# An attention-and-router kernel: overflow table built with the first constants, 16 buffers of row numbers, ranks after the state products, early row transposes in the last three rounds

## The chip, the cores and the metric

One Trainium2 chip, one of its cores. A core has a matrix engine (PE, its weight loads listed as PEld), a vector engine (DVE), a scalar engine (ACT), a general engine (POOL) and a sync engine (SP) that issues plain transfers; POOL issues the transfers that convert types or that go to rows named by an index. Each engine works off its own list of instructions in order. The metric is the device time of one execution in microseconds, lower is better; a change of 1% is about 2.7 us.

## The reference

Two stages. The first is linear attention with decay over 4 batches, 8 heads, 768 positions and 64 channels, worked in blocks of 64 positions:

```
intra = (qb @ kb^T * Dmask) @ vb
inter = (qb * lam_pow) @ kv_state
out[block] = intra + inter
kv_state = lam_block * kv_state + (kb * rev_pow)^T @ vb
```

Its output, transposed to 3072 tokens of 512 channels, is x of the second stage, a router with 8 experts:

```
logits = normalize(x) @ normalize(expert_emb).T / tau      # tau = 0.1
expert_idx = argmax(logits);  gate_w = softmax(logits)[expert_idx]
for e in range(8):                                         # w1[e]: 512x1024, w2[e]: 1024x512
    out[mask_e] = gate_w[mask_e] * (relu(x[mask_e] @ w1[e]) @ w2[e])
```

All inputs and the output are float32.

## The kernel before, in words

**Order.** The order of instructions on every engine is written out by hand (a manual schedule): the program text is walked once, and each engine gets its instructions in that order. Small steps of the router are hung into the attention rounds with `at(round, slot, step)`, and `run(i, slot)` puts them into the lists when round i comes to that slot. Semaphores are set by the framework where one engine needs another's result or buffer.

**Attention.** 24 rounds, i = 0 to 23, of 128 tokens each, six rounds to a batch. Round i transposes q and k for round i+2 (`pe_Tq`, `pe_Tk`), forms x against the embeddings for round i-1 (`pe_X`), forms the scores of round i+1 (`pe_ST`), and then fills the bank `o_ps` of round i: `pe_inter` (state times q, L354), `pe_kv` (the state's update, L380), `pe_O` (scores times v, L363). ACT copies the result to `xT` (`ev_O`), DVE updates the state, POOL scales k (`pool_ks`, L290). `o_ps` has one buffer, so the next round's `pe_inter` waits until every reader of the last `o_ps` is done.

**Router inside the rounds.** Tokens are ranked in eight groups, `[0..3] [4..7] [8..11] [12..15] [16,17] [18,19] [20,21] [22,23]`. For a group that ends at round n-1: one-hot choice `oh` on DVE in round n+1, then on PE the rank of each token within its expert (`pe_rank`: `ltri` and `ones` against `oh`, L469 to L474, into a free corner of `o_ps`), in round n+2 on DVE the row number (`rt_b`, L484 to L494), and then POOL scatters 128 rows at a time to a table in DRAM, `xs_dram` (`scatter`, L529). Once, after the first 16 tokens of rounds (`TA`), `pe_part` counts tokens per expert and `rt_part` (L504 to L508) turns the counts into a base for the later groups. `load_early` (round 20, on SP) then reads back the first 256 rows of the experts 0 to 2, after a small read `mark` that waits for the scatters of the first 16 rounds.

**Experts.** Rows come as three kinds: `a` (first 256 rows of the experts 0 to 2), `b` (their next 128), `f` (384 rows of the experts 3 to 7), and `q` (32 rows of each of four experts, in one block). For each piece PE transposes the rows (`xt_copy`, L598, copied to SBUF by ACT at L600; the last 32 columns by `add_q` on DVE, L735), then `pe_L1` (L753, relu by ACT at L755 and DVE at L757), then `pe_L2` (L787) whose result `put` scales on DVE into `y_sb` (L766). `put` first makes row numbers `xi` (`mask_rows`, L587, L589) and then POOL scatters `y_sb` to the output (L769). Order on PE: A0, A1, A2, B0, B1, B2, F3 to F7, with the `q` blocks between.

**Weights.** Each expert has four pieces of 512 KB in SBUF (float32 in DRAM, converted on the way), issued by POOL (`load_w`, L276), one list for all 32. Twelve are issued in the rounds, two more at the end of attention, and 18 between the output scatters, as the table `more` says. The first of these 18 stands behind `seen`, a copy on POOL that waits for rows of expert 3 (L779).

**Overflow.** `overs` (L807 to L818) makes from the counts a table of how many further tiles each expert needs; a branch at the very end reads it and does nothing here unless an expert has more than 416 rows. It starts with an `iota` on POOL, `pstart` (L807), which DVE reads at L813.

Of the kernel before, what the change touches and what calls it, by code (L numbers as in the profile page):

```python
# [11 lines left out]
FP32 = mybir.dt.float32  # L12
# [10 lines left out]
def kernel(  # L23
# [13 lines left out]
    P = 128  # L37
# [133 lines left out]
    lamb = const.tile([P, NC, HP], FP32, name="lamb")  # L171
    for c in range(NC):
        nc.vector.tensor_scalar(lamb[:, c, :], loglam_rows, float(c * 2 * P), None, op0=ALU.mult)
    lamq = const.tile([P, NC, 2, HP, P], FP32, name="lamq")

    def decays(c):
        for hp in range(HP):
# [49 lines left out]
    def last_constants():  # L227
        nc.gpsimd.memset(zrow, 0)
        nc.gpsimd.memset(zrow[:, :, DW : DW + 1], int(OOB_IDX))
        nc.gpsimd.tensor_copy(ident16, ident)  # L230
        nc.gpsimd.memset(ones16, 1.0)
        make_upper_triangular(nc, ltri, val=1.0, diag=False)
        nc.gpsimd.iota(rev, pattern=[[-1, E]], base=E, channel_multiplier=0,
                       allow_small_or_imprecise_dtypes=True)
        nc.gpsimd.iota(ebase[0], pattern=[[ROWS, E]], base=0, channel_multiplier=0,
                       allow_small_or_imprecise_dtypes=True)
        for t, n, base in ((row_a, 2, 0), (row_b, 1, CA), (row_f, GE, 0)):
            nc.gpsimd.iota(t, pattern=[[1, n]], base=base, channel_multiplier=n,
                           allow_small_or_imprecise_dtypes=True)
        for n in range(NQ):  # L240
            nc.gpsimd.iota(row_q[ds(CQ * n, CQ), :], pattern=[[0, 1]], base=GE * P,
                           channel_multiplier=1, allow_small_or_imprecise_dtypes=True)
        for n in range(4):
            nc.gpsimd.iota(tok_iota[ds(32 * n, 32), :], pattern=[[P, R]],
                           base=C * (n // 2) + n % 2, channel_multiplier=2)
        nc.gpsimd.memset(ohcum, 0.0)
        nc.gpsimd.memset(bump, 0.0)


    xps = ps2.tile([P, 2, 512], FP32, name="xps", tag="xps")  # L250
# [214 lines left out]
    def pe_rank(gi):  # L465
        nt = len(groups[gi])
        oh = rt[gi]["oh"]
        pc, pc3 = rank_of(gi)
        nc.tensor.matmul(pc, ltri, oh.rearrange("p k e -> p (k e)"), start=True, stop=False,  # L469
                         skip_group_check=True)  # L470
        nc.tensor.matmul(pc3, ones16, ohcum.unsqueeze(1).to_broadcast([P, nt, E]),
                         start=False, stop=(nt == 1), skip_group_check=True)
        for j in range(nt - 1):
            nc.tensor.matmul(pc3[:, j + 1 : nt, :], ones16,  # L474
                             oh[:, j : j + 1, :].to_broadcast([P, nt - 1 - j, E]),
                             start=False, stop=(j == nt - 2), skip_group_check=True)
# [16 lines left out]
        nc.vector.tensor_reduce(oc, d["oh"].rearrange("p k e -> p e k"), axis=AXL.X, op=ALU.add)  # L493
        nc.vector.tensor_tensor(ohcum, ohcum, oc, op=ALU.add)  # L494

    def pe_counts(dst):
        nc.tensor.matmul(dst, ones16, ohcum, start=True, stop=True, skip_group_check=True)

    def pe_part():
        pcs["a"] = bank["o"][:, 0, 2 * P + 64 : 2 * P + 64 + E]  # L500
        pe_counts(pcs["a"])

    def rt_part():
        nc.vector.tensor_copy(cnt_a, pcs["a"])  # L504
# [69 lines left out]
    def mask_rows(key):  # L574

        n = xe[key].shape[1]
        m = rsm.tile([P, GE], FP32, name="m", tag="m")[:, 0:n]
        kind, e = key
        if kind == "q":
            for r in range(NQ):  # L580
                nc.vector.tensor_scalar(m[ds(CQ * r, CQ)], row_q[ds(CQ * r, CQ), :],
                                        cnt[ds(CQ * r, CQ), NQ * e + r : NQ * e + r + 1], OOB_IDX,
                                        op0=ALU.is_ge, op1=ALU.mult)
        else:
            rows = {"a": row_a, "b": row_b, "f": row_f}[kind]
            c = cnt_a if kind == "a" else cnt
            nc.vector.tensor_scalar(m, rows, c[:, e : e + 1], OOB_IDX, op0=ALU.is_ge, op1=ALU.mult)  # L587
        xi[key] = rsm.tile([P, GE], I32, name="xi", tag="xi", bufs=4)
        nc.vector.tensor_tensor(xi[key][:, 0:n], xe[key][:, :, DW], m, op=ALU.max)  # L589

    def xt_copy(key, g0, g1, pst):
# [20 lines left out]
    for gi in range(GL):  # L612
# [3 lines left out]
        at(n + 1, "dve", rt_a2, gi)  # L616
        if groups[gi][0] == TA:
            at(n + 1, "pe", pe_part)
            at(n + 2, "dve", rt_part)
        at(n + 1, "pe", pe_rank, gi)  # L620
        if n + 2 < R:
            at(n + 2, "dve", rt_b, gi)
# [11 lines left out]
                at(min(n + 2 + late, R - 1), "pool", scatter, gi, j)  # L634
    at(0, "sp", fill)
    at(20, "sp", load_early)
    for i in (8, 10, 12, 14, 15, 16, 17, 20, 20, 21, 21, 22):
        at(i, "w", load_w, 1)

    def early_xT():  # L640
        xt_copy(("a", 0), 0, 2, ps.tile([P, DC * 2 * P], FP16, name="q_xtr", tag="q"))

    at(R - 2, "pe3", early_xT)

    act_q(0)
    pool_ks(0)
    for i in range(-2, R):
# [19 lines left out]
            ev_ST(i + 1)  # L667
        if i >= 0:
            new_o()
            run(i, "pe")  # L670
            pe_inter(i)
            pe_kv(i)
            pe_O(i)
            ev_O(i)
            state(i)
# [27 lines left out]
    mx = const.tile([P, 1], I32, name="mx")  # L703
    below = const.tile([P, E, R], FP32, name="below")
    ntile = const.tile([P, E], I32, name="ntile")
    pstart = const.tile([P, R], FP32, name="pstart")
    n_scat = [0]
    more = {1: 4, 2: 1, 3: 1, 4: 2, 5: 2, 6: 1, 7: 1, 8: 1, 9: 1, 11: 2, 12: 2}
    seen = const.tile([1, 1], I32, name="seen")
# [1 line left out]
    with (  # L711
        tc.tile_pool(name="wpool2", bufs=3) as wpool2,
        tc.tile_pool(name="moe_sb", bufs=2) as moe_sb,
        tc.tile_pool(name="moe_y", bufs=6) as moe_y,
        tc.tile_pool(name="ps_mx", bufs=1, space=bass.MemoryType.PSUM) as ps_mx,
        tc.tile_pool(name="ps_h", bufs=3, space=bass.MemoryType.PSUM) as ps_h,
        tc.tile_pool(name="ps_y", bufs=2, space=bass.MemoryType.PSUM) as ps_y,
# [42 lines left out]
        def put(y_ps, key, g):  # L760
# [15 lines left out]
            )  # L776

            if n_scat[0] == 1:
                nc.gpsimd.tensor_copy(seen, xe["f", NA][0:1, 0, DW : DW + 1])  # L779
            load_w(more.get(n_scat[0], 0))  # L780
            n_scat[0] += 1

# [21 lines left out]
            nc.vector.tensor_tensor(cnt, cp, bump, op=ALU.add)  # L804

        def overs():
            nc.gpsimd.iota(pstart, pattern=[[P, R]], base=0, channel_multiplier=0,  # L807
                           allow_small_or_imprecise_dtypes=True)
            nc.vector.tensor_scalar(last, cnt, -1.0, None, op0=ALU.add)
            nc.vector.tensor_scalar(over, cnt, float(-CE), 0.0, op0=ALU.add, op1=ALU.max)  # L810
            nc.vector.tensor_reduce(mx, over, axis=AXL.X, op=ALU.max)

            nc.vector.tensor_tensor(  # L813
                below, over.unsqueeze(2).to_broadcast([P, E, R]),
                pstart.unsqueeze(1).to_broadcast([P, E, R]), op=ALU.is_gt)
# [18 lines left out]
        rt_d(GL)  # L834
        for j in range(2):
            scatter(GL, j)
        for e in range(NA):
            load_b(e)
        load_xq(0)
        load_f(3)  # L840
        pe_xT(A[1], 0, 2)
        pe_L2(A[0], 0)
        counts()
        pe_L2(A[0], 1)
        pe_L1(A[1])
        pe_xT(A[2], 0, 2)
        pe_L2(A[1], 0)
        pe_L2(A[1], 1)
        pe_L1(A[2])
# [8 lines left out]
        for e in range(NA):  # L858
# [4 lines left out]
            else:  # L863
                pe_xT(F_[3], 0, 2)
            pe_L2(B_[e], 0)
        overs()
        pe_xT(F_[3], 2, 3)
        add_q(F_[3])
        for e in range(NA, E):
# [112 lines left out]
```

## Time and profile before

| what | value |
|---|---|
| time, median of 3 runs | 266.15 us (265.71 to 268.03) |
| profiled execution, own time | 263.92 us |
| its span | 262.0 us |
| PE busy | 221.4 us (84%) |
| DVE, ACT, POOL busy | 124.6, 127.6, 100.9 us |
| DMA | 49.76 MB, mean 190 GB/s |
| weight pieces | 32, 512 KB each in SBUF |

The profile shows one execution. Its own time is 1.92 us above its span, and 2.23 us under the median of the timed runs. A busy share is a mean over stages: attention runs to about 137 us, the experts from there to about 253 us, then the last output lands. In the rows below, an engine's idle time stands in brackets with the engine and the line that ended it.

### The profile page before, as it was taken

The numbers are of one execution on the slowest core, as the hardware profiler recorded it, in microseconds if no ns is written. First come the engines' busy times: TensorE is split into PE (matmuls) and PEld (weight loads), VectorE is DVE, ScalarE is ACT, GpSimd is POOL, SyncE is SP. The second block draws the span as 40 slices with busy tenths as digits, with TensorE's granted clock in tenths as the row PEclk, the third lists the DMA queues.
The fourth block names the chain that finished last, engine by engine and source line by source line (L and its number), as shares of the span: only waits on it lengthen the run. The fifth ranks groups of instructions, "written<-read, shape, count | busy, mean of one in ns | idle before, by whom it ended". The sixth has DMA issues, their size and how long they took to land.

```text
span 262.0 us, 7196 instructions
## 1 busy us (share of the span) xinstructions
PE 221.4 (84%) x2926; PEld 168.3 (64%) x2926; DVE 124.6 (48%) x413; ACT 127.6 (49%) x282; POOL 100.9 (39%) x143
## 2 busy tenths in 40 slices
PE   0799999997999997997889999970099999999960
PEld 0678897896888896886766776650045556565520
DVE  1274556657756667768744224531014433333340
ACT  5667555654566555654457555550034454372400
POOL 4481311354094195082455406425302813214050
PEclk9999999999999999999999999997569999999995
DMA  6999999988999899984799948999995999122130
GB/s 155 241 240 177 219 220 234 245 216 175 205 166 265 208 223 253 224 221 142 125 211 226 235 126 224 241 241 237 233 252 138 206 248 240 45 80 81 44 116 18
DMA packets 72589, 49.76 MB, mean 190 GB/s; under 512 B 52031, under 2 KB 64959, under 8 KB 72546
## 3 DMA queue, kind: packets, MB, share of 16 engines
q0 software_dynamic: 7840, 26.25, 43.8%
q1 hardware_dynamic: 64706, 22.96, 39.5%
q8 instruction: 25, 0.41, 0.7%
q14 instruction: 18, 0.15, 0.2%
HBM read 55.88 MB, written 10.61 MB: 254 GB/s over the span
## 4 chain that ended last, share of the span: by engine, by line
PE 33%; DMA 21%; issue 19%; DVE 10%; ACT 6%; POOL 6%; SPq 1%; POOLq 1%; DVEq 0%
DMA w_sb<-in_moe_w_dram 13%; PE s_ps L327 7%; PE o_ps L363 7%; DMA xs_dram<-xg,si 5%; PE xps L403 5%; POOL out_dram L769 5%; PE o_ps L380 4%; PE q_ps L302 3%; PE o_ps L354 3%; PE k_ps L315 2%; ACT xT L369 2%; DVE qT L304 2%; DMA qn<-in_q_dram 2%; DMA x_e<-xs_dram 2%; ACT qr L284 1%
## 5 line engine op out<-in xcount | busy, mean ns | idle before, releaser
L753 PE MATMUL h_ps<-xTe,w_sb 128*128 128x416 f16 (+2 forms) x352 | 50.3, 298 | 16.2 <-DVE xTe L735 15.2
L755 ACT ACTIVATE hT<-h_ps 128x384 f16<-128x384 f32 (+2 forms) x88 | 34.9, 402 | 49.7 <-PE h_ps L753 48.8
L753 PEld LDWEIGHTS <-w_sb 128*128 128x128 f16 x352 | 36.1, 114 | 30.3 <-issue 19.4
L769 POOL DMA_INDIRECT out_dram<-y_sb,xi x26 | 26.2, 1007 | 56.6 <-DVE y_sb L766 34.5
L529 POOL DMA_INDIRECT xs_dram<-xg,si x24 | 24.4, 1017 | 51.8 <-ACT kT L317 16.3
L787 PE MATMUL y_ps<-w_sb,hT 128*128 128x512 f16 x192 | 44.2, 379 | 0.0
L336 DVE TENSOR_TENSOR stm<-s_ps,step 64x512 f32<-64x512 f32 (+1 forms) x48 | 30.7, 676 | 10.2 <-PE s_ps L327 10.1
L290 POOL TENSOR_TENSOR ks<-kn,kdec 128x512 f32<-128x512 f32 x24 | 25.3, 1054 | 24.9 <-DMA kn<-in_k_dram 19.4
L766 DVE TENSOR_SCALAR y_sb<-y_ps,x_e 128x512 f32<-128x512 f32 x24 | 18.0, 750 | 31.7 <-PE y_ps L787 29.3
L787 PEld LDWEIGHTS <-hT 128*128 128x128 f16 x192 | 18.0, 98 | 18.7
L408 ACT ACTIVATE sq<-xps 128x512 f16<-128x512 f32 x24 | 14.3, 597 | 28.0 <-DVE z_sb L405 18.3
L403 PE MATMUL xps<-ien,xT 128*128 128x136 f32 x192 | 26.6, 281 | 1.6 <-ACT xT L369 1.4
L327 PE MATMUL s_ps<-qT,kT 64*64 64x128 f32 (+1 forms) x768 | 26.8, 259 | 0.3
L403 PEld LDWEIGHTS xps<-ien,xT 128*128 128x128 f32 x192 | 23.9, 190 | 2.4 <-ACT xT L369 2.2
L363 PE MATMUL o_ps<-stm,vn 128*64 128x128 f32 x384 | 25.3, 274 | 0.0
L757 DVE TENSOR_SCALAR hq<-h_ps 128x32 f16<-128x32 f32 x64 | 12.2, 191 | 26.1 <-ACT hT L755 25.0
L302 PE MATMUL q_ps<-ident,qr 128*128 128x128 f32 x96 | 16.7, 299 | 9.2 <-ACT qr L284 9.2
L327 PEld LDWEIGHTS s_ps<-qT,kT 64*64 64x64 f32 x768 | 21.0, 135 | 4.1 <-DVE qT L304 1.7
L369 ACT COPY xT<-o_ps 128x512 f32<-128x512 f32 x24 | 14.1, 587 | 18.2 <-PE o_ps L363 18.2
L276 POOL DMA_DIRECT2D w_sb<-in_moe_w_dram x32 | 18.1, 577 | 9.1 <-DMA w_sb<-in_moe_w_dram 6.6
L363 PEld LDWEIGHTS o_ps<-stm,vn 128*64 128x64 f32 x384 | 20.6, 137 | 0.7 <-issue 0.7
L304 DVE TENSOR_TENSOR qT<-q_ps,lamq 128x512 f32<-128x512 f32 x24 | 16.3, 678 | 9.5 <-PE q_ps L302 9.5
(127 smaller groups left out, 256.6 us busy)
## 6 DMA issues: line engine op xcount, KB each, us to landing
w_sb<-in_moe_w_dram POOLq DMA_DIRECT2D x32, 512.0 KB, 10.2
kn<-in_k_dram SPq DMA_DIRECT2D x24, 256.0 KB, 6.1
qn<-in_q_dram SPq DMA_DIRECT2D x12, 512.0 KB, 7.2
vn<-in_v_dram SPq DMA_DIRECT2D x24, 256.0 KB, 7.3
x_e<-xs_dram SPq DMA_DIRECT2D x5, 387.0 KB, 6.3
x_e<-xs_dram SPq DMA_DIRECT2D x3, 258.0 KB, 4.0
xs_dram<-zrow SPq DMA_DIRECT2D x1, 516.0 KB, 8.3
out_dram<-y_sb,xi POOLq DMA_INDIRECT x26, 3.6
```

The lines of the kernel that those rows point to most:

```text
L290: nc.gpsimd.tensor_tensor(ks[i], kn[i], kdec[:, i % RB].unsqueeze(2).to_broadcast([P, H, D]), op=ALU.mult)
L302: nc.tensor.transpose(t[:, hp, :], qr[j][:, s, 2 * hp : 2 * hp + 2, :].rearrange("p h d -> p (h d)"), ident)
L304: nc.vector.tensor_tensor(qT[j][:, :, :, s, :].rearrange("p a h i -> p h a i"), t.rearrange("p h (a i) -> p h a i", i=C // 2), lamq[:, j % ...
L327: nc.tensor.matmul(sb[ds(C * c, C), h2, hp, c:2, :], kT[i][ds(64 * h2, 64), hp, ds(C * c, C)], q_of(i, hp, c)[ds(64 * h2, 64)], start=(hp ...
L336: nc.vector.tensor_tensor(stm[i][0:n, :, :, c], sb[0:n, :, :, c], step[0:n, c].rearrange("p s i -> p (s i)").unsqueeze(1).unsqueeze(1) .to ...
L363: nc.tensor.matmul(o_at(h2, u, b2), vn[i][:, 2 * hp + h2, :], stm[i][:, h2, hp], start=(i % RB == 0 and b2 == 0), stop=True, skip_group_ch ...
L403: nc.tensor.matmul(xz[:, a // 2, a % 2, :], xT_of(t, a), ien[:, a, :], start=(a % 2 == 0), stop=True, skip_group_check=True)
L529: nc.gpsimd.indirect_dma_start(out=xs_views[groups[gi][j]], out_offset=bass.IndirectOffsetOnAxis(ap=slot_i[gi][:, j : j + 1], axis=0), in_ ...
L753: nc.tensor.matmul(h_ps[:, 0:n], w_cols(w, c, fc), xTe[key][:, c, 0:n], start=(c == 0), stop=(c == DC - 1))
L755: nc.scalar.activation(hT[key][:, fc, 0:nm], h_ps[:, 0:nm], AF.Relu)
L769: nc.gpsimd.indirect_dma_start(out=out_views[n_scat[0]], out_offset=bass.IndirectOffsetOnAxis(ap=xi[key][:, g : g + 1], axis=0), in_=y[:], ...
L787: nc.tensor.matmul(y_ps, hT[key][:, fc, ds(P * g, P)], w[:, fc, :], start=(fc == 0), stop=(fc == FC - 1))
```

## The change

Several edits at once. `pstart` is made with the other constants at the start, instead of inside `overs`, and `overs` runs after the last `pe_L2` of F3 instead of after B2. The row numbers `xi` get 16 buffers instead of 4, the results `y_sb` 8 instead of 6 (room for them comes from `lamq`, now in a pool that closes with attention). In each round `pe_rank` and `pe_part` stand behind `pe_inter` and `pe_kv` instead of ahead of them (the `start` flags follow). `rt_part` runs at the middle of round 19 instead of early in round 20. One weight piece is issued in round 18 instead of round 22. The transposes of A0, A1 and A2 stand at the ends of the rounds 21, 22 and 23; before, A0's stood at the end of round 22 and the other two among the expert products. On SP the rows of `q` go ahead of those of B1 and B2, and `seen` waits for B2's rows instead of F3's.

```diff
-    lamq = const.tile([P, NC, 2, HP, P], FP32, name="lamq")
+    lamq = wk.tile([P, NC, 2, HP, P], FP32, name="lamq", tag="lamq", bufs=1)
...
+    pstart = const.tile([P, R], FP32, name="pstart")
...
+        nc.gpsimd.iota(pstart, pattern=[[P, R]], base=0, channel_multiplier=0,
+                       allow_small_or_imprecise_dtypes=True)
...
-        nc.tensor.matmul(pc, ltri, oh.rearrange("p k e -> p (k e)"), start=True, stop=False,
+        own = gi >= GL - 1 or (groups[gi][-1] + 2) % RB == 0
+        nc.tensor.matmul(pc, ltri, oh.rearrange("p k e -> p (k e)"), start=own, stop=False,
...
-        xi[key] = rsm.tile([P, GE], I32, name="xi", tag="xi", bufs=4)
+        xi[key] = rsm.tile([P, GE], I32, name="xi", tag="xi", bufs=2 * E)
...
-            at(n + 2, "dve", rt_part)
+            at(n + 1, "mid", rt_part)
...
-    for i in (8, 10, 12, 14, 15, 16, 17, 20, 20, 21, 21, 22):
+    for i in (8, 10, 12, 14, 15, 16, 17, 18, 20, 20, 21, 21):
         at(i, "w", load_w, 1)
 
-    def early_xT():
-        xt_copy(("a", 0), 0, 2, ps.tile([P, DC * 2 * P], FP16, name="q_xtr", tag="q"))
-
-    at(R - 2, "pe3", early_xT)
+    def early_xT(e, tag):
+        xt_copy(("a", e), 0, CA // P, ps.tile([P, DC * CA], FP16, name="xtr_early", tag=tag))
+
+    for e, tag in enumerate("qsq"):
+        at(R - NA + e, "pe3", early_xT, e, tag)
...
             new_o()
-            run(i, "pe")
             pe_inter(i)
             pe_kv(i)
+            run(i, "pe")
             pe_O(i)
...
-        tc.tile_pool(name="moe_y", bufs=6) as moe_y,
+        tc.tile_pool(name="moe_y", bufs=8) as moe_y,
...
-                nc.gpsimd.tensor_copy(seen, xe["f", NA][0:1, 0, DW : DW + 1])
+                nc.gpsimd.tensor_copy(seen, xe["b", NA - 1][0:1, 0, DW : DW + 1])
...
-        for e in range(NA):
-            load_b(e)
+        load_b(0)
         load_xq(0)
+        load_b(1)
+        load_b(2)
         load_f(3)
-        pe_xT(A[1], 0, 2)
...
-        pe_xT(A[2], 0, 2)
...
             pe_L2(B_[e], 0)
-        overs()
         pe_xT(F_[3], 2, 3)
         add_q(F_[3])
...
             pe_L2(F_[e], 2)
+            if e == NA:
+                overs()
```

On DVE, between the result of B2 (`y_sb`) and the first relu of F3 (`hq`), before:

```order
L766 TENSOR_SCALAR y_sb<-y_ps,x_e 128x512
L809 TENSOR_SCALAR last<-cnt 128x8
L810 TENSOR_SCALAR over<-cnt 128x8
L811 TENSOR_REDUCE mx<-over 128x1
L813 TENSOR_TENSOR below<-over,pstart 128x192
L817 TENSOR_REDUCE ntile_f<-below 128x8
L818 CAST ntile<-ntile_f 128x8
L735 COPY xTe<-xq 128x4x32
L757 TENSOR_SCALAR hq<-h_ps 128x32 x8
```

The same place in the changed kernel, from the relu of B2 on:

```order
L761 TENSOR_SCALAR hq<-h_ps 128x32 x8
L591 TENSOR_SCALAR m<-row_b,cnt 128x1
L593 TENSOR_TENSOR xi<-x_e,m 128x1
L770 TENSOR_SCALAR y_sb<-y_ps,x_e 128x512
L739 COPY xTe<-xq 128x4x32
L761 TENSOR_SCALAR hq<-h_ps 128x32 x8
```

The six steps of the overflow table no longer stand between B2's result and `xTe`, the last columns of F3's rows; they come after the third `y_sb` of F3.

On PE in round 9, a round with ranks, behind the scores of round 10, before:

```order
L469 LDWEIGHTS ltri
L469 MATMUL o_ps<-oh,ltri 128x32
L471 LDWEIGHTS ones_153
L471 MATMUL o_ps<-ohcum,ones_153 128x32
...
L354 MATMUL o_ps<-qT,kv_1_149 64x128 x8
L380 MATMUL o_ps<-vn,ks 64x64 x8
L363 MATMUL o_ps<-stm_145,vn 64x128 x8
L302 MATMUL q_ps<-ident,qr 128x128 x4
```

and in the changed kernel:

```order
L357 MATMUL o_ps<-qT,kv_1_149 64x128 x8
L383 MATMUL o_ps<-vn,ks 64x64 x8
L473 LDWEIGHTS ltri
L473 MATMUL o_ps<-oh,ltri 128x32
...
L366 MATMUL o_ps<-stm_145,vn 64x128 x8
L305 MATMUL q_ps<-ident,qr 128x128 x4
```

The ranks moved behind the 16 state products; what follows `pe_O`, the transposes of q, stays where it was.

On POOL from round 18 to the end of attention (`ks` is the scaled k, `xs_dram` a scatter of router rows, `w_sb` a weight piece), before:

```order
L529 DMA xs_dram<-xg,si 24576x258 x2
L290 TENSOR_TENSOR ks<-kn,kdec 128x512
L529 DMA xs_dram<-xg,si 24576x258 x2
L290 TENSOR_TENSOR ks<-kn,kdec 128x512
L529 DMA xs_dram<-xg,si 24576x258 x2
L276 DMA w_sb<-in_moe_w_dram 128x2048 x4
L529 DMA xs_dram<-xg,si 24576x258 x2
L276 DMA w_sb<-in_moe_w_dram 128x2048
L529 DMA xs_dram<-xg,si 24576x258 x2
L276 DMA w_sb<-in_moe_w_dram 128x2048 x2
```

and in the changed kernel:

```order
L533 DMA xs_dram<-xg,si 24576x258 x2
L279 DMA w_sb<-in_moe_w_dram 128x2048
L293 TENSOR_TENSOR ks<-kn,kdec 128x512
L533 DMA xs_dram<-xg,si 24576x258 x2
L293 TENSOR_TENSOR ks<-kn,kdec 128x512
L533 DMA xs_dram<-xg,si 24576x258 x2
L279 DMA w_sb<-in_moe_w_dram 128x2048 x4
L533 DMA xs_dram<-xg,si 24576x258 x4
L279 DMA w_sb<-in_moe_w_dram 128x2048 x2
```

One weight piece moved from between the last scatters to a place ahead of the two scatters of round 19, for which `mark`, and so the early rows, wait.

## Rows read from the trace of the kernel before

**Rows 1.** Windows: stretch and length, busy us of each engine, clock, DMA share, GB/s

```profile
137.00:175.20 38.20, 37.13 (x316) 27.30 (x314) 15.25 (x65) 21.72 (x61) 14.61 (x20) 1.00 0.90 213
175.20:190.50 15.30, 0.14 (x3) 0.07 (x2) 2.11 (x9) 0.58 (x1) 7.04 (x10) 0.67 1.06 239
190.50:205.80 15.30, 15.30 (x105) 7.87 (x106) 5.16 (x19) 6.06 (x11) 3.40 (x4) 0.89 0.82 186
205.80:217.30 11.50, 11.50 (x70) 6.68 (x69) 4.18 (x14) 5.47 (x10) 5.09 (x8) 1.00 1.04 243
```

**Rows 2.** Waits from 140 us on: total us, times, longest us

```profile
PE h_ps L753 <- DVE xTe L735: 15.2, 1, 15.2
DVE below L813 <- POOL pstart L807: 9.5, 1, 9.5
DVE xi L589 <- DMA out_dram<-y_sb,xi: 5.0, 1, 5.0
```

**Rows 3.** Timeline of PE among the experts: start us, us, instruction, idle before

```profile
142.08 0.61 PE L598 MATMUL xtr<-ident,x_e 128*128 128x128 f16 x8
142.53 1.89 PE L787 MATMUL y_ps<-w_sb,hT 128*128 128x512 f16 x8
...
173.19 1.89 PE L787 MATMUL y_ps<-w_sb,hT 128*128 128x512 f16 x8
...
190.46 7.47 PE L753 MATMUL h_ps<-xTe,w_sb 128*128 128x416 f16 x32 [15.16 <-DVE xTe L735]
...
205.79 5.79 PE L753 MATMUL h_ps<-xTe,w_sb 128*128 128x416 f16 x32
```

**Rows 4.** Timeline of DVE from B2's result to F3's last columns

```profile
178.65 0.74 DVE L766 TENSOR_SCALAR y_sb<-y_ps,x_e 128x512 f32<-128x512 f32 x1
...
189.27 0.36 DVE L813 TENSOR_TENSOR below<-over,pstart 128x192 f32<-128x192 f32 x1 [9.53 <-POOL pstart L807]
...
190.12 0.19 DVE L735 COPY xTe<-xq 128x128 f16<-128x128 f16 x1
```

**Rows 5.** Timeline of POOL: the first of the 18 weight issues, and the iota

```profile
159.42 2.20 POOL L276 DMA_DIRECT2D w_sb<-in_moe_w_dram  x4
...
189.03 0.20 POOL L807 IOTA pstart<- 128x24 f32 x1
```

**Rows 6.** Chain of waits, 155 to 190 us: start us, us, what

```profile
159.18 0.18 POOL seen L779
...
161.06 13.96 DMA w_sb<-in_moe_w_dram
...
176.80 12.95 DMA w_sb<-in_moe_w_dram
```

**Rows 7.** Timeline of PE in attention: rounds 9, 20, 22 and the last

```profile
62.14 0.19 PE L469 MATMUL o_ps<-oh,ltri 128*128 128x32 f16 x1 [1.63 <-DVE oh L442]
...
119.17 0.67 PE L354 MATMUL o_ps<-qT,kv 64*64 64x128 f32 x16 [1.29 <-DVE t L484]
...
127.36 1.19 PE L403 MATMUL xps<-ien,xT 128*128 128x136 f32 x8 [0.69 <-ACT xT L369]
...
136.19 1.19 PE L403 MATMUL xps<-ien,xT 128*128 128x136 f32 x8 [0.74 <-ACT xT L369]
```

**Rows 8.** Timeline of all engines in rounds 9, 19 and 20

```profile
63.34 1.06 ACT L284 COPY qr<-qn 128x1024 f32<-128x1024 f32 x1
...
116.97 1.64 DVE L507 TENSOR_SCALAR bump<-bump 128x3 f32<-128x3 f32 x1
117.53 1.05 POOL L290 TENSOR_TENSOR ks<-kn,kdec 128x512 f32<-128x512 f32 x1
```

**Rows 9.** Issues of 91.8, 93.6 and 119.6 us: KB each, us to landing

```profile
w_sb<-in_moe_w_dram POOLq DMA_DIRECT2D x1, 512.0 KB, 8.1
...
xs_dram<-xg,si POOLq DMA_INDIRECT x1, 7.0
...
x_e<-xs_dram SPq DMA_DIRECT2D x1, 258.0 KB, 2.7
```

More of the change, by code (lines that the diff above doesn't have):

```diff
@@ L494, in rt_b, with pe_counts @@
         nc.vector.tensor_tensor(ohcum, ohcum, oc, op=ALU.add)
-    def pe_counts(dst):
-        nc.tensor.matmul(dst, ones16, ohcum, start=True, stop=True, skip_group_check=True)
+    def pe_counts(dst, own=True):
+        nc.tensor.matmul(dst, ones16, ohcum, start=own, stop=True, skip_group_check=True)
     def pe_part():
         pcs["a"] = bank["o"][:, 0, 2 * P + 64 : 2 * P + 64 + E]
-        pe_counts(pcs["a"])
+        pe_counts(pcs["a"], own=False)
     def rt_part():
@@ L705 @@
     ntile = const.tile([P, E], I32, name="ntile")
-    pstart = const.tile([P, R], FP32, name="pstart")
     n_scat = [0]
@@ L806, in overs @@
         def overs():
-            nc.gpsimd.iota(pstart, pattern=[[P, R]], base=0, channel_multiplier=0,
-                           allow_small_or_imprecise_dtypes=True)
             nc.vector.tensor_scalar(last, cnt, -1.0, None, op0=ALU.add)
```

## The prediction

> **What bounds the kernel now.** I read the windows first: busy time of each engine by stretch. From 137 to 175.2 us PE is busy 37.1 of 38.2 us, and from 190.5 on it is busy without a gap; between them lie 15.3 us in which PE works 0.14 us [rows 1]. So among the experts PE is the bound, with one hole. The waits name the hole: F3's first product waited 15.2 us for `xTe`, the last columns of F3's rows, which DVE copies; DVE waited 9.5 us for `pstart` and before that 5.0 us for a row-number buffer `xi` that an output scatter still held [rows 2]. The timeline of DVE has the steps in a row: B2's result at 178.65 us, the table's first steps, then `below` at 189.27 us, as soon as POOL had made `pstart` at 189.03 us, and the copy at 190.12 us [rows 4, 5]. The `iota` itself takes 0.20 us; it was late because it stands in POOL's list behind weight issues and scatters. The chain of waits shows that backlog: the weight piece issued at 161.06 us landed 13.96 us later, the one of 176.80 us 12.95 us later [rows 6]. In attention PE is the bound as well, with small gaps [rows 7].
>
> **The stall goes.** In the changed kernel DVE makes `xi` without a wait (16 buffers, 16 uses) and goes from B2's result straight to the copy. B2's product starts at 173.19 us and takes 1.89 us [rows 3], DVE's scaling takes 0.74 us and the copy 0.19 us [rows 4]; with 0.3 us of steps between them F3's first product can start at 173.19 + 1.89 + 0.74 + 0.19 + 0.3 = 176.3 us instead of 190.46 us [rows 3]. **-14.2 us**, bounds -12 (DVE held 2 us by something that I don't see) and -14.5.
>
> Three things could be late next, and each has to be placed.
> - *F3's own data.* Its first weights are issued at the end of attention, behind the second last pair of router scatters, in both versions; its rows landed by 159.18 us, when `seen` ran [rows 6]. Both are far ahead of 176 us.
> - *The next weights.* 18 pieces are issued from 159.42 us on [rows 5]. The fourth landed at 161.06 + 13.96 = 175.02 us, the ninth at 176.80 + 12.95 = 189.75 us [rows 6]: 2.95 us a piece, scatters between them included, with the DMA engines full (share 1.06 [rows 1]). That stream doesn't depend on PE while POOL has results to scatter. From the fourth at about 173 us (`seen` comes some 2 us earlier, see below), the 8th lands at 185, the 14th at 202, the last at 173 + 14 x 2.95 = 214 us. PE, with F3 at 176.3, reaches F4 after 13.6 us (205.79 - 190.46 = 15.33 us less the 1.7 us below), at 189.9 us, and each next expert 11.5 us later [rows 1]: F4 needs the fourth (189.9 against 173), F5 the 8th (201 against 185), F7's second product the last (230 against 214). The least slack is 16 us, so the stream stays hidden.
> - *The result buffers.* Result n needs scatter n-8. The first result of F4 (number 13) comes about 197 us and needs scatter 5, which stands behind the 8th piece, 186 us; with 6 buffers it would need scatter 7, behind three more pieces, about 194 us. Six would just have done here; eight leave 11 us.
>
> **The clock.** The granted clock was 0.67 in the hole and 0.89 behind it, 1.00 before and later [rows 1]: F3's 32 products took 7.47 us, F4's same 32 took 5.79 us [rows 3]. With a gap of 1 us instead of 15 I expect it to stay at 1.00, as it did from 137 to 175.2 us, where the gaps of PE come to 1.1 us in all [rows 1]. **-1.7 us**, bounds -1.7 and 0.
>
> **Early transposes.** A1's and A2's leave the expert stage, where PE has no gap: 142.53 - 142.08 = 0.45 us each [rows 3], -0.9 us. In the rounds 21 and 23 they fall into the waits for ACT's copy of `xT`, 0.69 and 0.74 us [rows 7], which cover 0.45 us. ACT's extra copies stand behind `xT` in its list, where ACT then waits for the next x from PE and DVE. If the cover is gone, the 0.9 us come back: bounds -0.9 and 0, taken **-0.9**.
>
> **Ranks and `rt_part`.** In round 9 PE waited 1.63 us for `oh` [rows 7]; the state products, two sets of some 0.6 us (the first is the 0.67 us of round 20), could fill 1.2 us of that. But the next transposes of q wait for ACT's `qr`, which ended at 63.34 + 1.06 = 64.40 us [rows 8] and follows the same late DVE, so PE would only wait later. I take **0**; bounds -1.5 and +0.4 (the ranks, and the row numbers behind them, come 0.6 to 1.2 us later where nothing waited). `rt_part` is different: in round 20 `pe_inter` waited 1.29 us for DVE to read the old `o_ps` [rows 7], and DVE had spent 1.64 us in the small step `bump` while POOL ran `ks` [rows 8]. Moved into round 19's middle, it starts right behind the state's update, ahead of the q copy of round 20, and clear of that `ks`. That gives between -1.3 (all of the wait) and 0 (the `xT` copy of round 20 is late anyway); I take **-0.7**.
> The row shows `bump`, a step of 3 numbers a row, ending at 118.61 us, just after `ks` at 118.58 us [rows 8]. The Trainium skill, SBUF — State Buffer, Who interferes with whom, says that a `tensor_scalar` in a two-port mode, or a `tensor_tensor` with two SBUF inputs, can be shut out for the whole length of a GpSimd instruction; the row agrees. By that page `ks` of round 20 would now catch one of the ranks' `tensor_tensor` steps instead, and the gain would be 0.2 and not 0.7 us, the sum 0.5 us less.
>
> **The moved overflow table.** Its steps (three of about 0.15 us, and 189.27 to 190.12 us for the rest [rows 4]) now lie between F3's last result and F4's first relu columns, 1.3 us of DVE. PE has three `h_ps` buffers, 2.1 us of products (three of 5.79 / 8 us [rows 3]), and DVE scales F3's last result for 0.74 us [rows 4] just as F4 begins, some 0.2 us behind: 0.2 + 0.74 + 1.3 and 0.2 for the first relu columns make 2.45 against 2.1. **+0.4**, bounds 0 and +1.4.
>
> **The piece moved to round 18, the order on SP, `seen`.** The last router scatters lose a weight issue ahead of them (about 0.6 us of POOL, and one piece of traffic, 2.95 us), so B's rows, `seen` and the weight stream come 2 to 3 us earlier; nothing on PE waits for them, 0. In exchange the two scatters of round 19 stand behind a piece: such a scatter took 7.0 us to land behind a piece that took 8.1 us [rows 9]. A0's rows were issued at 119.6 us, once those scatters had landed, and took 2.7 us [rows 9], to 122.3 us; I put them 2 to 4 us later, at 124.5 to 126.5 us. PE will ask for them at the end of round 21, 127.36 - 0.69 = 126.7 us [rows 7] less the 0.7 us of `rt_part`, 126.0. Taken **0**, bounds 0 and +3. The `iota` at the start (0.20 us), `lamq` and the buffers: 0, POOL waits for k there.
>
> **Sum.** -14.2 - 1.7 - 0.9 - 0.7 + 0.4 = -17.1 us. The profiled execution of 263.92 us becomes 246.8 us, its span 244.9. The timed median lies 2.2 us above that execution; the same step from it gives 266.15 - 17.1 = **249.0 us**.
>
> **Rivals.**
> - *Early rows come late.* PE works in order, so it would stand in round 21 until A0's rows land, and everything after it shifts. For it: both numbers above lie within 1 us; against: the DMA engines have idle time just there. Price 1 to 4 us: 250 to 253 us.
> - *The weight stream takes the stall's place, and the kernel gets slower.* Place: PE ahead of F7's second product. The last piece would have to land after 230 us, so the 14 pieces behind the fourth must take (230 - 173) / 14 = 4.1 us each; from there on every 0.1 us costs 1.4 us, and at 5.3 us a piece the 17 us are used up. At 5.5 us it would be 269 us. Against: 2.95 us with the engines already full, and PE's reads don't touch DRAM. A mild form (4.2 to 4.5 us) gives 251 to 255 us.
> - *The change doesn't remove the wait*: something else that is ready at about 190 us holds F3. The waits show nothing of the kind, and F3's weights and rows are early. 263 to 266 us.
> - *More comes of it*: all of `rt_part`, some of the ranks, 246 to 247 us.
>
> **How the numbers follow.** Forecast (248 to 250): 0.62. More: 0.14. Late rows: 0.13. Weight stream, mild: 0.05; slower than before: 0.02. Wait not removed: 0.03. The rest: 0.01. A range of 245.5 to 253 us leaves out the slower and unremoved cases and the ends of the others, some 0.13 in all. About 1%, 2.7 us, is what a measurement of this kernel can tell from no change: faster by more 0.95, within 0.03, slower 0.02.
>
> **What would show it.** Right: PE's wait ahead of F3's first product about 1 us, ended by DVE's copy; no wait for `pstart` or for `xi`; F3's 32 products in 5.8 us and the clock at 1.00 throughout; F4 13.6 us after F3. `rt_part`: `pe_inter` of round 20 with no wait. Ranks: the wait in round 9 gone and the one for `qr` longer by as much. Wrong: a PE wait for `x_e` at the end of round 21, a weight load of PE that waits for a transfer between F4 and F7, or `y_sb` waiting for a scatter.

## The result, and the profile after

The changed kernel takes 252.56 us (250.2 to 254.58, 4 runs), the kernel before 266.11 us beside it (265.71 to 268.03); the ratio is 0.9448, 95% interval 0.9361 to 0.9535. That is -13.6 us where -17.1 was forecast; 249.0 us was the forecast, its range 245.5 to 253. The ratio leaves out the changed kernel's longest run, 254.58 us, as one of the slower state that some executions of either kernel show. The profiled execution took 252.15 us, its span is 250.2.

Windows of the changed kernel, columns as in [rows 1]:

```profile
140.00:178.90 38.90, 36.80 (x305) 26.88 (x304) 16.57 (x68) 20.65 (x61) 16.87 (x23) 1.00 0.93 221
178.90:192.50 13.60, 13.60 (x104) 7.56 (x105) 5.09 (x19) 6.06 (x11) 6.32 (x8) 1.00 1.06 239
192.50:204.50 12.00, 11.70 (x70) 6.65 (x69) 5.36 (x20) 5.48 (x10) 5.32 (x7) 1.00 1.06 274
204.50:227.40 22.90, 22.90 (x137) 13.28 (x136) 8.37 (x28) 10.96 (x20) 7.42 (x8) 1.00 0.68 181
```

The hole is gone: PE is busy from F3 (178.9 us) on but for 0.3 us, and the clock is 1.00 where [rows 1] had 0.67 and 0.89. DMA is full in F3 and F4 (1.06), and no transfer holds PE. PE's timeline answers to [rows 3] and [rows 7]:

```profile
105.02 0.66 PE L305 MATMUL q_ps<-ident,qr 128*128 128x128 f32 x4 [1.02 <-ACT qr L287]
...
110.42 1.09 PE L406 MATMUL xps<-ien,xT 128*128 128x136 f32 x8
...
112.46 1.02 PE L357 MATMUL o_ps<-qT,kv 64*64 64x128 f32 x14
113.78 0.31 PE L383 MATMUL o_ps<-vn,ks 128*64 128x64 f32 x2 [0.30 <-issue]
114.48 0.63 PE L383 MATMUL o_ps<-vn,ks 128*64 128x64 f32 x14 [0.39 <-issue]
...
120.51 0.67 PE L357 MATMUL o_ps<-qT,kv 64*64 64x128 f32 x16 [1.21 <-DVE t L488]
...
136.21 0.17 PE L478 MATMUL r_ps<-oh,ones 128*128 128x8 f16 x1
...
139.63 1.19 PE L406 MATMUL xps<-ien,xT 128*128 128x136 f32 x8 [1.69 <-ACT xT L372]
...
178.88 5.79 PE L757 MATMUL h_ps<-xTe,w_sb 128*128 128x416 f16 x32 [0.81 <-DVE xTe L739]
...
192.53 2.27 PE L757 MATMUL h_ps<-xTe,w_sb 128*128 128x416 f16 x12
195.10 3.68 PE L757 MATMUL h_ps<-xTe,w_sb 128*128 128x416 f16 x20 [0.30 <-DVE hq L761]
```

F3 starts after a wait of 0.81 us, ended by DVE's copy, runs its 32 products in 5.79 us, and F4 follows 13.65 us later: the expert stage as forecast. Attention is not. In round 19 the products with the state stand 0.30 and 0.39 us with no releaser shown (`issue`); in round 20 `pe_inter` still waits 1.21 us, as in [rows 7]; behind round 23 the last x waits 1.69 us for `xT`, where it was 0.74. The timeline of DVE and POOL there, which answers to [rows 8]:

```profile
114.62 1.28 DVE L339 TENSOR_TENSOR stm<-s_ps,step 64x512 f32<-64x512 f32 x2 [2.21 <-remote]
...
117.67 1.60 DVE L509 TENSOR_SCALAR bump<-cnt_a 128x3 f32<-128x3 f32 x1
118.19 1.05 POOL L293 TENSOR_TENSOR ks<-kn,kdec 128x512 f32<-128x512 f32 x1
...
137.21 0.17 DVE L488 TENSOR_TENSOR t<-r_ps,ebase 128x16 f32<-128x16 f32 x1 [1.25 <-PE r_ps L478]
```

`stm`, DVE's step on PE's scores, starts after 2.21 us of idle time, ended by an event for which the profile has no instruction on record (`remote`). `rt_part` did move, but `bump` again lasts until `ks` has ended. And DVE starts on the ranks of round 23 at 137.21 us, 0.8 us after PE's last rank product (136.21 + 0.17).

Cut into stages by PE's rows (X18 is x of tile 18 at 110.42, X23 that of tile 23 at 139.63), with a second profile of the same changed kernel, `again`, that is shown below:

| stage, us | before | changed, first measurement | changed, `again` |
|---|---|---|---|
| start to X18 | 110.37 | 110.42 | 109.75 |
| X18 to X23 (rounds 19 to 23) | 25.82 | 29.21 | 25.61 |
| X23 to F3 | 54.27 | 39.25 | 39.04 |
| F3 to F4 | 15.33 | 13.65 | 13.64 |
| F4 to F5 | 11.48 | 11.93 | 11.67 |
| F5 to F7 | 22.95 | 22.96 | 22.96 |
| F7 to the end | 21.78 | 22.78 | 21.63 |
| span | 262.0 | 250.2 | 244.3 |

So the profiled step is -11.8 us in the first measurement and -17.7 us in the second, and the 5.9 us between lie in rounds 19 to 23 (3.6), behind F7 (1.15), ahead of X18 (0.7) and in small pieces.

### The profile page after: what moved, and what is told of

It is laid out like the page before. It is cut to its first block, busy times and chain, and to the rows that moved or that the text cites. A ratio compares the mean times of both kernels' runs of the same rounds, so it can differ in the third digit from the quotient of the medians.

```text
span 250.2 us, 7198 instructions
## 1 busy us (share of the span) xinstructions
PE 221.9 (89%) x2926; PEld 169.8 (68%) x2926; DVE 123.9 (50%) x413; ACT 127.2 (51%) x282; POOL 100.7 (40%) x143
## 3 DMA queue, kind: packets, MB, share of 16 engines
q1 hardware_dynamic: 64706, 22.96, 41.8%
## 4 chain that ended last, share of the span: by engine, by line
PE 57%; DVE 13%; issue 12%; ACT 7%; POOL 4%; DMA 2%; another core or an unknown queue 1%; POOLq 1%; SPq 0%; DVEq 0%
PE y_ps L791 10%; PE h_ps L757 10%; PE s_ps L330 7%; PE o_ps L366 7%; PE xps L406 6%; PE o_ps L383 4%; POOL out_dram L773 4%; PE q_ps L305 4%; PE o_ps L357 3%; PE k_ps L318 3%; ACT xT L372 2%; DVE qT L307 2%; DMA qn<-in_q_dram 2%; ACT qr L287 2%; DVE y_sb L770 2%
## 5 line engine op out<-in xcount | busy, mean ns | idle before, releaser
L757 PE MATMUL h_ps<-xTe,w_sb 128*128 128x416 f16 (+2 forms) x352 | 48.8, 292 | 2.4 <-DVE xTe L739 0.8
L293 POOL TENSOR_TENSOR ks<-kn,kdec 128x512 f32<-128x512 f32 x24 | 25.3, 1054 | 25.3 <-DMA kn<-in_k_dram 17.7
L366 PE MATMUL o_ps<-stm,vn 128*64 128x128 f32 x384 | 26.1, 275 | 0.1
L305 PEld LDWEIGHTS q_ps<-ident,qr 128*128 128x128 f32 x96 | 10.7, 147 | 15.4 <-issue 10.8
```

The lines of the kernel that those rows point to most:

```text
L293: nc.gpsimd.tensor_tensor(ks[i], kn[i], kdec[:, i % RB].unsqueeze(2).to_broadcast([P, H, D]), op=ALU.mult)
L305: nc.tensor.transpose(t[:, hp, :], qr[j][:, s, 2 * hp : 2 * hp + 2, :].rearrange("p h d -> p (h d)"), ident)
L366: nc.tensor.matmul(o_at(h2, u, b2), vn[i][:, 2 * hp + h2, :], stm[i][:, h2, hp], start=(i % RB == 0 and b2 == 0), stop=True, skip_group_ch ...
L757: nc.tensor.matmul(h_ps[:, 0:n], w_cols(w, c, fc), xTe[key][:, c, 0:n], start=(c == 0), stop=(c == DC - 1))
```

## The experiments

They were made in three measurements, the second to the fourth, each of four kernels beside new runs of the kernel before.

**Second measurement (before 263.97 us).** `again`: nothing edited.

> The changed kernel once more, nothing edited, to see which of its new waits return. The theory that round 19's extra 1.4 us (state products held at 112.5 to 114.5 us in the first profile) belongs to one execution: x of round 20 and the state products of round 19 are not late here, and the span is 1 to 1.5 us shorter. The rival, that the order of the change makes it: the same stall of 1 to 1.5 us in round 19 again. Both expect the wait of PE for xT in round 23 (1.69 us) and the wait of pe_inter in round 20 (1.2 us) again. Time 250 to 253 us.

246.38 us, ratio 0.9345 (0.9302 to 0.9388), -17.6 us. PE's timeline of `again`:

```profile
109.75 1.09 PE L406 MATMUL xps<-ien,xT 128*128 128x136 f32 x8
...
111.79 0.66 PE L357 MATMUL o_ps<-qT,kv 64*64 64x128 f32 x14
112.38 0.69 PE L383 MATMUL o_ps<-vn,ks 128*64 128x64 f32 x16
...
132.84 0.17 PE L478 MATMUL r_ps<-oh,ones 128*128 128x8 f16 x1
...
135.36 1.19 PE L406 MATMUL xps<-ien,xT 128*128 128x136 f32 x8 [0.79 <-ACT xT L372]
...
174.40 5.79 PE L757 MATMUL h_ps<-xTe,w_sb 128*128 128x416 f16 x32 [0.81 <-DVE xTe L739]
188.04 5.98 PE L757 MATMUL h_ps<-xTe,w_sb 128*128 128x416 f16 x32
```

And its timeline of DVE and POOL:

```profile
112.09 1.28 DVE L339 TENSOR_TENSOR stm<-s_ps,step 64x512 f32<-64x512 f32 x2 [0.35 <-PE s_ps L330]
...
115.54 0.17 DVE L509 TENSOR_SCALAR bump<-cnt_a 128x3 f32<-128x3 f32 x1
...
117.25 1.36 DVE L494 CAST si<-sf 128x2 int32<-128x2 f32 x1
117.52 1.06 POOL L293 TENSOR_TENSOR ks<-kn,kdec 128x512 f32<-128x512 f32 x1
...
133.04 0.17 DVE L488 TENSOR_TENSOR t<-r_ps,ebase 128x16 f32<-128x16 f32 x1 [0.45 <-PE r_ps L478]
```

No stop in round 19, and `stm` waits 0.35 us, for PE's scores; `bump` takes 0.17 us, well ahead of `ks`, and `pe_inter` of round 20 has no wait; DVE takes up the ranks of round 23 0.03 us after the last of them, and `xT` is waited for 0.79 and not 1.69 us. Both theories had expected those two waits to return and a time of 250 to 253 us; neither came. The losses of the first profile were not the change's order as such.

`ranks23`: the ranks of round 23 alone in front.

```diff
             new_o()
+            if i == R - 1:
+                run(i, "pe")
             pe_inter(i)
             pe_kv(i)
-            run(i, "pe")
+            if i < R - 1:
+                run(i, "pe")
```

> The changed kernel with the rank products of round 23 alone back ahead of the products with the state. My theory: they end about 2.4 us earlier, DVE's first step on them and the Exp that stands ahead of the xT copy on ACT come earlier too, PE's wait for xT of round 23 falls from 1.69 to about 0.5 us, and the time falls by 1.2 to 1.6 us against the changed kernel. The rival, that x comes late for another reason (the early transposes' copies on ACT or DMA traffic): wait and time stay, within 0.4 us.

246.59 us, no difference, where my theory had 1.2 to 1.6 us less. By its rows round 23 (X22 to X23) takes 4.01 us against 4.31 in `again`, and the wait for `xT` is 0.19 us: the mechanism is there, but worth 0.3 us when nothing else is late.

`piece22`: the weight piece of round 18 back in round 22.

```diff
-    for i in (8, 10, 12, 14, 15, 16, 17, 18, 20, 20, 21, 21):
+    for i in (8, 10, 12, 14, 15, 16, 17, 20, 20, 21, 21, 22):
```

> The changed kernel with the weight piece of round 18 back in round 22. My theory: the piece of round 18 only delays the router scatters of round 19 and A0's rows behind them; the rows are issued at about 120 instead of 124.3 us, the 0.9 us that round 21 grew by are given back, round 19 stays as it is: 0.6 to 1.0 us less than the changed kernel. The rival, that this piece also holds rounds 19 and 20: 2 to 2.5 us less. The other rival, that the last scatters and the experts' rows need the early piece: the same or up to 1 us more.

246.52 us, no difference, where I had expected 0.6 to 1.0 us less; rounds 19 and 20 take 10.93 us in place of 11.13, round 21 5.33 in place of 5.34. The piece costs 0.2 us, and not where I expected it.

`table_early`: the kernel before with one edit.

```diff
...
         nc.gpsimd.memset(bump, 0.0)
+        nc.gpsimd.iota(pstart, pattern=[[P, R]], base=0, channel_multiplier=0,
+                       allow_small_or_imprecise_dtypes=True)
...
         def overs():
-            nc.gpsimd.iota(pstart, pattern=[[P, R]], base=0, channel_multiplier=0,
-                           allow_small_or_imprecise_dtypes=True)
```

> The kernel before with one edit: the table's row of constants is made among the first constants; 4 row-number buffers, the order of the steps and all else as before. My theory, in which the wait for the constants and the one for the row-number buffer stand one behind the other: DVE gets B2's buffer at 178.6 us as before, makes the result, does the table in 1.3 us and the copy, F3 starts at about 181 instead of 190.5 us, and the clock loses about 1 us less: 9.5 to 11 us faster than the kernel before, some 5 us short of what both edits give. The rival, that the buffer's wait is hidden behind another limit and the constants were all of it: 14 to 16 us faster. The other, that the buffer or a transfer holds F3 anyway: under 4 us.

253.39 us, ratio 0.959 (0.9543 to 0.9636), -10.6 us: my theory's. Timelines of DVE and of PE in it:

```profile
177.35 0.16 DVE L592 TENSOR_TENSOR xi<-x_e,m 128x1 int32<-128x1 int32 x1 [5.20 <-DMA out_dram<-y_sb,xi]
177.43 0.74 DVE L768 TENSOR_SCALAR y_sb<-y_ps,x_e 128x512 f32<-128x512 f32 x1
...
178.44 0.35 DVE L813 TENSOR_TENSOR below<-over,pstart 128x192 f32<-128x192 f32 x1
...
179.29 0.19 DVE L737 COPY xTe<-xq 128x128 f16<-128x128 f16 x1
...
179.62 7.24 PE L755 MATMUL h_ps<-xTe,w_sb 128*128 128x416 f16 x32 [5.73 <-DVE xTe L737]
```

Two locks stood one behind the other: with the constants there, DVE still waits 5.2 us for the row-number buffer, then the table runs at once, and PE's wait is 5.73 in place of 15.16 us [rows 3]. The clock is another matter: I had expected about 1 us back, and F3 to F4 takes 15.10 us, 0.2 less than before. This kernel has before's attention, and X18 to X23 takes it 25.84 us, as in before's profile.

**Third measurement (before 263.35 us).** `again2`: nothing edited.

> The changed kernel once more, nothing edited, with new runs of the kernel before beside it. Theory: the forecast step of -17.1 us is the change's own, and the first measurement's -13.6 us holds 3 to 4 us of stops of that measurement; expected -16 to -18.5 us, no stop of the state products in round 19 and no wait of pe_inter in round 20. The rival, that the step itself varies from measurement to measurement: anything between -13 and -18 us, with stops at other places.

246.37 us, ratio 0.9363 (0.9324 to 0.9403), -17.0 us; X18 to X23 is 25.61 us again.

`rows4`: 4 row-number buffers.

```diff
-        xi[key] = rsm.tile([P, GE], I32, name="xi", tag="xi", bufs=2 * E)
+        xi[key] = rsm.tile([P, GE], I32, name="xi", tag="xi", bufs=4)
```

> The changed kernel with 4 row-number buffers in place of 16. Theory, that the buffer's wait is a second lock behind the constants: DVE waits for xi ahead of B2's result until about 176 to 177 us, F3 starts 2.5 to 4 us later and runs its first products at a lower clock: 3.5 to 5.5 us slower than the changed kernel. The rival, that the order of the table alone explains what table_early fell short by: within 0.7 us of the changed kernel.

249.28 us, ratio 0.9467 (0.9429 to 0.9505): 2.9 us slower than `again2`. Its DVE and PE:

```profile
174.48 0.16 DVE L593 TENSOR_TENSOR xi<-x_e,m 128x1 int32<-128x1 int32 x1 [3.58 <-DMA out_dram<-y_sb,xi]
...
175.55 5.79 PE L757 MATMUL h_ps<-xTe,w_sb 128*128 128x416 f16 x32 [2.91 <-DVE xTe L739]
```

The lock is real, but opens earlier than in `table_early`, so the 2.9 us are less than the 3.5 that I gave as the least. The rows are those of its fastest execution (247.11 us), in which the clock holds through the 2.91 us. That it held in the others is not shown: two of them (249.16 and 249.4 us) have a mean granted clock of 0.979 and 0.981, where the executions of `again2` have 0.986 to 0.991.

`ranks_front`: all ranks back in front, with their own start flags.

```diff
             new_o()
+            run(i, "pe")
             pe_inter(i)
             pe_kv(i)
-            run(i, "pe")
```

> The changed kernel with all rank products back ahead of the products with the state. Prediction's theory, that PE waits for q's copy instead: the wait for oh returns in the rounds 9 and 17 (1.1 to 1.6 us each) and the wait for qr falls by as much; round 23 gains 0.3 us; within 0.5 us of the changed kernel. The rival, that the ranks behind the state products save what PE waited before: 1 to 2 us slower. The other, that they cost what the first profile seemed to show (round 23): 1 to 1.6 us faster.

246.56 us, ratio 0.9368 (0.933 to 0.9406): no difference, the prediction's theory. PE in round 17 shows the trade:

```profile
101.83 0.19 PE L473 MATMUL o_ps<-oh,ltri 128*128 128x32 f16 x1 [1.13 <-DVE oh L445]
...
104.14 0.66 PE L305 MATMUL q_ps<-ident,qr 128*128 128x128 f32 x4 [0.41 <-ACT qr L287]
```

In `again` the same two waits are 0.67 and 1.02 us: what the state products cover is waited for at q's copy. In round 9 the wait for `oh` is only 0.42 us here, with the ranks in front; `table_early`, with before's attention, has the same 0.42, so the 1.63 us of [rows 7] belonged to that execution. Rounds 19 and 20 take 11.57 us here against 11.13 in `again`, and round 23 takes 4.01 against 4.31: behind the state products the ranks gain 0.4 us at the one place and lose 0.3 at the other.

`part_round20`: `rt_part` back in round 20.

```diff
-            at(n + 1, "mid", rt_part)
+            at(n + 2, "dve", rt_part)
```

> The changed kernel with rt_part back in round 20. Theory (the term of -0.7 us): DVE's small steps stand behind q's copy of round 20 and one of them is shut out while POOL makes ks; PE's wait ahead of pe_inter returns with 0.9 to 1.3 us, and the kernel is 0.4 to 1.1 us slower than the changed one. The rival, that the xT copy of round 20 is late anyway: within 0.3 us.

246.24 us, ratio 0.9345 (0.9311 to 0.938): no difference, the rival by time. By rows, rounds 19 and 20 take 11.55 us against 11.13 in `again`. The step caught by `ks` was another one:

```profile
115.92 0.17 DVE L509 TENSOR_SCALAR bump<-cnt_a 128x3 f32<-128x3 f32 x1
...
116.76 1.64 DVE L490 TENSOR_TENSOR t<-t,oh 128x16 f32<-128x16 f32 x1
117.31 1.05 POOL L293 TENSOR_TENSOR ks<-kn,kdec 128x512 f32<-128x512 f32 x1
```

PE's products wait only for the step before, `t<-o_ps`, so `pe_inter` doesn't wait.

**Fourth measurement (before 267.15 us).** The unedited changed kernel was not timed in it; `results6`, which differs from it in two buffers, stands in for it below. `table_in_front`: the table's steps back ahead of F3's copy, constants and buffers as changed.

```diff
+        overs()
         pe_xT(F_[3], 2, 3)
         add_q(F_[3])
...
-            if e == NA:
-                overs()
```

> The changed kernel with the table's steps back between B2's result and F3's copy; its constants stay early and the row-number buffers stay 16. Theory: the 1.3 us of small steps lie on the path again, F3's wait grows from 0.81 to 2.1 us, F4 loses its 0.2 us of stretch: 0.9 to 1.3 us slower than the changed kernel, the clock at 1.00. The rival, that the order of the table was the lock and not its constants: 5 us slower or more. The other, that ACT's copy or a transfer ends that wait anyway: within 0.4 us.

253.86 us without one execution of 453.54 us (254.39 with it), ratio 0.9519 (0.9469 to 0.9569), 1.6 us over `results6`, whose interval it overlaps by a little. F3's wait is 2.26 us and F4 loses its stretch, +1.2 us by rows, as expected (0.9 to 1.3):

```profile
180.40 5.79 PE L757 MATMUL h_ps<-xTe,w_sb 128*128 128x416 f16 x32 [2.26 <-DVE xTe L739]
194.05 5.79 PE L757 MATMUL h_ps<-xTe,w_sb 128*128 128x416 f16 x32
```

`iota_late`: the `iota` back inside the table's function, the table behind F3, buffers as changed.

```diff
         nc.gpsimd.memset(bump, 0.0)
-        nc.gpsimd.iota(pstart, pattern=[[P, R]], base=0, channel_multiplier=0,
-                       allow_small_or_imprecise_dtypes=True)
...
         def overs():
+            nc.gpsimd.iota(pstart, pattern=[[P, R]], base=0, channel_multiplier=0,
+                           allow_small_or_imprecise_dtypes=True)
```

> The changed kernel with the iota back inside the table's function; the table stays behind F3 and the row-number buffers stay 16. Theory: the iota then stands in POOL's list behind the 13th output scatter and its two weight pieces and runs at about 200 us, DVE waits for it from 189 us on with F4's relu columns behind it, PE stops three h_ps tiles into F4: 9 to 11.5 us slower than the changed kernel, of which 1 to 1.5 us is the clock. The rival, that POOL has caught up by then: within 1 us.

264.83 us, ratio 0.9918 (0.9891 to 0.9946), 12.6 us over `results6`: nearly the whole gain is gone, more than the 9 to 11.5 us expected. Its POOL, DVE and PE:

```profile
203.40 0.19 POOL L809 IOTA pstart<- 128x24 f32 x1
203.63 0.36 DVE L815 TENSOR_TENSOR below<-over,pstart 128x192 f32<-128x192 f32 x1 [9.14 <-POOL pstart L809]
...
204.73 6.04 PE L755 MATMUL h_ps<-xTe,w_sb 128*128 128x416 f16 x20 [9.26 <-DVE hq L759]
```

The 13th output scatter and its pieces stand ahead of the `iota`, and the hole only moves from F3 into F4. F4's last 20 products take 6.04 us, where the changed kernel's take 3.68: 2.4 us lost behind the gap, at a clock of 0.67 for 7.3 us, where I had expected 1 to 1.5. Of the three edits the early constants are the main one.

`results6`: 6 result buffers.

```diff
-        tc.tile_pool(name="moe_y", bufs=8) as moe_y,
+        tc.tile_pool(name="moe_y", bufs=6) as moe_y,
```

> The changed kernel with 6 result buffers in place of 8. The prediction's estimate, that six would just have done: within 0.5 us, no wait of y_sb for a scatter in F4. The rival, that the scatters' landings behind the weight pieces are later than estimated: y_sb waits 1 to 4 us in F3 or F4, and PE's two y_ps tiles pass it on: 1 to 3 us slower.

252.23 us, ratio 0.9442 (0.9404 to 0.9479), that of the changed kernel in the first measurement (0.9448); no wait of `y_sb` for a scatter in F3 or F4. By its rows six would have done; the unedited kernel's time beside it is missing. PE shows the first measurement's stop of round 19, at the same place:

```profile
113.61 0.38 PE L383 MATMUL o_ps<-vn,ks 128*64 128x64 f32 x4 [0.28 <-issue]
114.35 0.58 PE L383 MATMUL o_ps<-vn,ks 128*64 128x64 f32 x12 [0.37 <-issue]
...
139.94 1.19 PE L406 MATMUL xps<-ien,xT 128*128 128x136 f32 x8 [1.68 <-ACT xT L372]
```

`three_small`: the edits of `ranks23` and `piece22`, and a third.

```diff
                 pe_xT(F_[3], 0, 2)
+                add_q(F_[3])
             pe_L2(B_[e], 0)
         pe_xT(F_[3], 2, 3)
-        add_q(F_[3])
```

> The changed kernel with three small edits at once: rank products of round 23 in front, the weight piece of round 18 back in round 22, F3's copy by DVE ahead of B2's result. Theory, from the stage times of the runs before: -0.3 us in round 23, -0.2 us in rounds 19 and 20, and -0.15 us ahead of F3, where ACT's copy ends next: 0.65 us less than the changed kernel, which 6 runs can barely tell. The rival, that they return nothing: within 0.2 us.

251.38 us, ratio 0.9417 (0.9373 to 0.9461), 0.85 us under `results6`, inside the spread. It is 15.8 us faster than the kernel before and has the lowest median of the fourth measurement, but that it beats the changed kernel is not shown. F3 now waits for ACT:

```profile
139.05 1.19 PE L406 MATMUL xps<-ien,xT 128*128 128x136 f32 x8 [1.17 <-ACT xT L372]
...
177.98 4.20 PE L760 MATMUL h_ps<-xTe,w_sb 128*128 128x416 f16 x23 [0.67 <-ACT xTe L604]
```

## Why the prediction came out as it did

- **The stall and the early transposes** (-14.2 and -0.9): right. X23 to F3 shrank by 15.0 us (first measurement) and 15.2 us (`again`) against 15.1. The part of the transposes alone, from `table_early` with its longer wait taken off, is 39.04 - (44.83 - 5.73 + 0.81) = -0.9 us. Not costed was the third lock, that the table would again be first in DVE's list: `table_in_front` puts it at 1.2 us.
- **The clock** (-1.7): right, F3 to F4 is 1.68 us shorter.
- **The moved table** (+0.4): F4 is stretched by 0.45 us in the first measurement, by 0.19 in `again`.
- **Ranks** (0): right in the time, and round 17 trades one wait for the other as forecast. But the 0 is also a gain of 0.4 us in rounds 19 and 20 set against 0.3 us that round 23, which I left out, pays (`ranks_front`, and `ranks23` for the second). In the first profile, where DVE took the ranks up 0.8 us late, round 23 took 5.21 us against before's 4.00.
- **`rt_part`** (-0.7): the way was right, the size was not. Rounds 19 and 20 take 11.13 us in `again` and 11.83 in `table_early`, a difference of 0.7, but three edits that touch these rounds lie between the two kernels. Put back alone, `rt_part` costs 0.4 us there (`part_round20`, 11.55), the ranks cost 0.4 (`ranks_front`, 11.57), and the piece of round 18 gives back 0.2 (`piece22`, 10.93); that they add up to the forecast 0.7 is luck. In the first measurement the stop of round 19 pushed `rt_part` back under `ks`, and it gave nothing. What POOL shuts out is told by ends that agree: `bump` ended 0.03 us after `ks` in the first profile (119.27 and 119.24), the cast to `si` 0.03 us after it in `again` (118.61 and 118.58), `t` 0.04 us after it in `part_round20` (118.40 and 118.36). The loss is handed to another step, and costs nothing only where nobody waits for that one. The Trainium skill, SBUF — State Buffer, Who interferes with whom, says that `tensor_scalar` and casts in a two-port mode, and a `tensor_tensor` with both inputs in SBUF, can be shut out for a whole GpSimd instruction, the ports going to whichever issues first; the three rows are one of each kind and agree on the first point. On the second they don't as recorded: each of the three starts 0.27 to 0.55 us before `ks` and is held all the same, and no row shows why. The 0.4 us that the move measured lies between the 0.2 that the prediction worked out by that page and the 0.7 that it took.
- **The piece, SP's order, `seen`** (0): 0.2 us for the piece by rows, nothing in the time. The early rows were in time or, in `again2` and `ranks23`, 0.2 us late.
- **The sum** in the two quicker measurements, the second and the third, -17.1 forecast and -17.6 and -17.0 measured, owes part of its closeness to luck: in `again` rounds 19 to 23 gave 0.2 us where 0.7 was forecast, and 0.6 us came ahead of X18, where before's profile had its long wait in round 9.
- **The step that failed is the last one of the sum**, "the same step from it gives": I took the 2.2 us between before's profile and its timed median as common to both kernels. Before stands at 264.0 and 263.4 us in the second and third measurement and at 266.1 and 267.2 in the first and fourth, 2 to 4 us apart; the changed kernel stands at 246.4 twice, and at 252.6 in the first (with 6 buffers at 252.2 in the fourth), 6 us apart. The record gives the chip of the last three: 0, 7 and 5, the slower one on chip 5; the first one's isn't given. No chip was used twice there, so whether the level goes with the chip or with the moment is not tested. The step of -17.1 us is what both quick measurements show (-17.6 and -17.0); in the others it is -13.6 and, with 6 buffers, -14.9. Before's profile, at 263.92 us, reads like a quick one: X18 to X23 is as in `table_early`, and its X18 is 1.4 us later than there, of which 1.2 are the wait in round 9. So I put a quick profile and a slower timed median into one sum: the step between them was 2.2 us for the kernel before, and for the changed one it measured 6.
- What these slower measurements slow is seen in the rows: all five profiles of them show the stop of round 19, between 113.2 and 114.7 us, with `stm` behind 2.2 us of idle time without a releaser on record, and none of the other eight does; rounds 19 to 23 take 28.9 to 29.7 us in the five and 25.3 to 26.0 in the eight. Where DVE follows PE it starts late (0.8 us behind the ranks of round 23 in the first profile, 0.03 in `again`). The edits of `three_small` don't remove the stop, so the piece of round 18 and the ranks of round 23 are not its cause. Why PE and DVE start late there stays open, and so does why the kernel before loses less: its hole could swallow a late attention, but that is not shown, as no profile of it in a slower measurement is at hand.

## What to carry to other kernels

When a wait goes, look down the same engine's list for the next lock before pricing the gain: here constants, buffers and the table's own steps stood one behind the other, and the first edit alone gave 10.6 of 17 us. A tiny instruction on an engine whose list also holds transfers' issues (the 0.2 us `iota`) belongs where that list is empty, not where its result is first used. And a step from one profile is good for measurements like that profile: time the kernel before next to it, since two kernels need not move together: here one stood 2 to 4 us apart between measurements and the other 6.

## What was not expected of the hardware

A PE gap of 2.91 us (`rows4`) and of 2.26 us (`table_in_front`) left the clock as it was in the profiled executions, F3's products taking 5.79 us; behind 5.73 us (`table_early`) and 9.26 us (`iota_late`) it was lower. For the two short gaps this is not shown beyond that one execution each: two other executions of `rows4` have a mean granted clock of 0.979 and 0.981, two of `table_in_front` 0.979 and 0.98, where the profiled ones have 0.988 and 0.986. Windows of `table_early` from its gap on:

```profile
173.80:179.60 5.80, 0.09 (x2) 0.01 (x1) 2.02 (x9) 0.59 (x1) 3.17 (x4) 0.96 1.06 255
179.60:186.80 7.20, 7.18 (x34) 4.04 (x35) 1.23 (x7) 3.44 (x7) 2.28 (x4) 0.79 1.06 232
186.80:194.70 7.90, 7.90 (x73) 3.84 (x72) 4.23 (x13) 2.63 (x4) 4.04 (x5) 1.00 1.07 246
```

The fall comes mostly after PE has started again (0.79, a mix of the levels 1.2 and 2.4 GHz), and costs 1.46 us from F3 to F4. Behind the longer gap of `iota_late` it cost the 2.4 us given there.
